# Query-weight means taken off by GpSimd, three loads on ScalarE's queue, key weights on two queues, and a new order

## The chip, the core and the metric

The kernel runs on one core of a Trainium2 chip. The core has five engines with separate instruction streams: TensorE (PE: matmuls and transposes into PSUM), VectorE (DVE), ScalarE (ACT), GpSimd (POOL) and SyncE (SP), which here only issues DMAs. ScalarE can issue DMAs too. The metric is the device time of one execution in microseconds.

## The reference

One block of a transformer, in bf16, for 2048 tokens of width 640, with 32 heads of width 20 and a gated layer of width 1536. `ln` is a layer norm without weights.

```python
q, k, v = split_heads(ln(x) @ wqkv)
pq, pk = q @ w_phi[h], k @ w_phi[h]                 # per head, 20 x 20
phi_q = concat(softmax(pq), softmax(-pq))           # 40 features
phi_k = concat(softmax(pk), softmax(-pk))
kv, z = sum_s phi_k * v, sum_s phi_k
o = (phi_q @ kv) / (phi_q @ z + 1e-6)
h = x + o @ wo
g, u = ln(h) @ w_gate, ln(h) @ w_up
out = h + (g * u) @ w_down
```

## The kernel before

The tokens lie in 16 tiles of 128, and the width of 640 in 5 chunks of 128. The kernel is a list of operations (`Prog.op`), each with its engine, what it reads and writes, and an expected length. Each operation belongs to a named unit (`U("...")`). `ORDER` gives, for each engine, a fixed list of unit names, and each name in it stands for the next operation of that unit on that engine, in the order in which the program created them (`place`, line 216). Every engine runs its list strictly in order and waits on semaphores where an operation depends on another engine's. `place` also simulates the list with the expected lengths to choose buffers and semaphores; its landing times of DMAs (line 252) are used in that simulation alone.

The stages, with the unit names:

- **Key weights ("wk", "x0" to "x4").** The layer norm's mean is folded into the weights, and `w_phi` is multiplied into them. The rows of Wk arrive in five blocks of 128 rows (`Wnat`, lines 512 to 515, unit "in"). For each block PE sums the columns (line 662) and turns the block with five transposes (line 656). Blocks 0 and 1 are copied out raw by VectorE and ScalarE (lines 693 and 696), since the mean is known only after block 4; blocks 2 to 4 are copied out later with the mean taken off (lines 708 and 711: unit "wk" again). The rounds x0 to x4 multiply by a band matrix `Phi` (six matmuls each, line 674); x0 and x1, which used raw blocks, take a second set of six with the broadcast negative mean. `evac` (line 751) copies each round to `Wp`, by ScalarE in rounds 0, 2 and 4.
- **Value weights ("wv", "c0" to "c4").** Two loads, column sums by PE, and VectorE takes the means off.
- **Token tiles.** `xT` is x transposed by the DMA (`load_xT`: the first four tiles in unit "in", then "lT4" to "lT15"). "s0", "s2", "s4", "s8" and "s12" work out 1/std for 2, 2, 4, 4 and 4 tiles: PE and VectorE make sums, and seven small operations on GpSimd make `rs`, `nrs` and `mv`. s12 takes its squares on ScalarE from `x_all`, the untransposed x, whose last quarter is "lx3".
- **Keys and values ("k", "K", "v").** PE projects a tile (10 matmuls of 320 columns), VectorE takes the largest absolute value, ScalarE writes two exponentials; then "K": sums by VectorE, scaling by GpSimd (line 827, 2.36 us a tile).
- **Query weights ("lwq", "t0" to "t4", "wm", "y0" to "y4").** Wq arrives twice: by a plain load (lwq, into `Wnat` again) for the column means, and transposed by the DMA (t0 to t4, into `WT`). "wm": 25 one-column matmuls sum the columns, and ScalarE writes the negative means, broadcast to 128x640, into `nmu`. Each round y multiplies `WT` by `Phi` (six matmuls) and adds `nmu` times `Phi` (six more).
- **Key sums ("A0" to "A14", "Aout"), queries ("q", "Q"), numerators ("n"), Wo ("wo0" to "wo4", "h"), the gated layer ("f") and its way down ("d", "e").** PE works through these for the rest of the span. "wo" sums Wo's rows on ScalarE (line 561), "h" needs Wo and x.

There are four PSUM buffers of two banks, shared by all PE stages. DMAs of one engine leave in the order of its list; SP issues all but Wrows, the small `w_phi` load, which ScalarE issues. SP's list begins "in" x 11 (key weights, value weights, four token tiles), then token tiles, x's last quarter (lx3), more tiles, Wq transposed and plain, Wo, and the gated layer's weights.

Of the kernel before, what the change touches and what calls it, by code (L numbers as in the profile page):

```python
# [376 lines left out]
def _build(ctx, nc, A_x, A_wqkv, A_w_phi, A_wo, B_w_gate, B_w_up, B_w_down, out):  # L377
# [136 lines left out]
    for c in range(NC):  # L514
        load_wnat(1, (c, c + 1))
# [588 lines left out]
```

## Time and profile before

| what | us |
|---|---|
| median of three runs | 283.45 (283.43 to 284.15) |
| the profiled execution | 281.24 |
| span within it, first to last instruction | 279.4 |
| PE busy | 274.6 (98% of the span) |
| VectorE, ScalarE, GpSimd busy | 165.5, 133.4, 106.3 |
| granted TensorE clock | 1.00 |

Busy time by stretch of the span, in us:

| stretch | PE | VectorE | ScalarE | GpSimd | DMA share |
|---|---|---|---|---|---|
| 0 to 7 | 5.68 | 1.62 | 1.99 | 3.54 | 0.71 |
| 7 to 13.7 | 6.51 | 6.16 | 3.15 | 2.61 | 1.02 |
| 20 to 30 | 10.00 | 9.86 | 8.34 | 7.92 | 1.16 |
| 40 to 50 | 10.00 | 9.76 | 9.70 | 8.99 | 0.98 |
| 60 to 70 | 10.00 | 10.00 | 8.96 | 9.92 | 0.29 |
| 70 to 80 | 9.45 | 8.49 | 5.22 | 5.04 | 1.05 |
| 100 to 150 | 50.00 | 35.27 | 22.83 | 13.02 | 0.65 |

A matmul's end is modelled in the profile, and matmuls are pipelined, so small gaps of PE do not show. The share of the DMA engines is summed over 16 engines and can come out a little above 1. The chain of waits is followed back from the last instruction; before 13.7 us it consists of SP's DMA issues and one token tile's transfer.

### The profile page before, as it was taken

What the parts mean: (1) busy time and instruction counts of PE and PEld (TensorE: products, weight loads), DVE (VectorE), ACT (ScalarE), POOL (GpSimd) and SP (SyncE); (2) the same over time, 40 slices, a digit from 0 to 9 for tenths busy, and PEclk for the clock granted to TensorE, in tenths of its full rate; (3) what the DMA queues carried; (4) which work ended last, traced back from release to release, by engine and by line L of the source; (5) the groups of instructions that cost most, each with busy time, mean ns of one, the idle gap of its engine ahead of it and who ended that gap; (6) DMA issues with size and microseconds to landing.
All of it is one profiled execution on the core that took longest, in us unless ns stands there. A gap on an engine that the chain in (4) does not pass through costs nothing.

```text
span 279.4 us, 5540 instructions
## 1 busy us (share of the span) xinstructions
PE 274.6 (98%) x2257; PEld 187.7 (67%) x2257; DVE 165.5 (59%) x313; ACT 133.4 (48%) x227; POOL 106.3 (38%) x156
## 2 busy tenths in 40 slices
PE   8999999999999999999999999999999999999996
PEld 7777778778878888877746655676454444456773
DVE  2999999999899798688528474431141132315011
ACT  2477999998566346363271432401444342410321
POOL 5348899999620322233300680002521034000321
PEclk9999999999999999999999999999999999999999
DMA  7989989404964378946530065561210001000112
GB/s 192 166 170 140 214 125 397 137 2 94 302 78 94 74 180 150 280 99 91 122 73 2 7 136 72 116 98 45 72 49 0 0 0 49 0 0 2 70 48 72
DMA packets 65241, 28.08 MB, mean 100 GB/s; under 512 B 55744, under 2 KB 63936, under 8 KB 65216
## 3 DMA queue, kind: packets, MB, share of 16 engines
q1 hardware_dynamic: 64560, 27.70, 45.8%
q8 instruction: 18, 0.29, 0.5%
q10 hardware_dynamic: 656, 0.03, 0.2%
q14 instruction: 7, 0.06, 0.1%
HBM read 11.82 MB, written 2.62 MB: 52 GB/s over the span
## 4 chain that ended last, share of the span: by engine, by line
PE 94%; SPq 3%; DMA 2%; DVE 1%; issue 0%
PE ps L568 93%; SPq L469 2%; DMA xT<-in_A_x_dram 2%; SPq L465 1%; PE ps L480 0%; DVE outb L1010 0%; DVE KVsb L893 0%; DVE rden L927 0%; DVE KVsb L896 0%
## 5 line engine op out<-in xcount | busy, mean ns | idle before, releaser
L568 PE MATMUL ps<-phik,Wgu 128*128 128x512 bf16 (+1 forms) x600 | 107.6, 336 | 0.0
L568 PEld LDWEIGHTS ps<-phik,Wgu 128*128 128x128 bf16 x600 | 58.2, 98 | 43.6 <-DVE phik L969 1.2
L969 DVE TENSOR_TENSOR phik<-ps,gate 128x512 bf16<-128x512 f32 (+1 forms) x60 | 34.0, 575 | 61.2 <-PE ps L568 60.3
L568 PE MATMUL ps<-Wp,xT 128*128 128x320 bf16 x480 | 68.4, 299 | 0.0
L967 ACT ACTIVATE gate<-ps 128x512 bf16<-128x512 f32 (+1 forms) x60 | 30.1, 512 | 70.4 <-PE ps L568 56.5
L568 PE MATMUL ps<-vaug,phik 128*128 128x320 bf16 (+3 forms) x544 | 60.2, 270 | 0.0
L568 PEld LDWEIGHTS ps<-Wp,xT 128*128 128x128 bf16 x480 | 46.2, 98 | 17.1
L568 PEld LDWEIGHTS ps<-vaug,phik 128*128 128x128 bf16 x544 | 43.4, 97 | 15.9
L985 POOL TENSOR_TENSOR outb<-t,x_all 128x640 bf16<-128x640 f32 x12 | 16.8, 1397 | 88.0 <-ACT t L982 85.7
L827 POOL TENSOR_TENSOR phik<-phik,Rk 128x1280 bf16<-128x1280 bf16 x16 | 37.3, 2357 | 0.7 <-DVE nb L809 0.6
L982 ACT ACTIVATE t<-ps,mh,rs 128x640 f32<-128x640 f32 x12 | 10.6, 882 | 41.4 <-PE ps L568 41.4
L806 DVE TENSOR_REDUCE ps<-ps 128x1 f32<-128x640 f32 x32 | 26.2, 819 | 3.5 <-PE ps L568 3.1
L846 DVE TENSOR_REDUCE Sq<-eq 128x64 f32<-128x1280 bf16 x16 | 23.5, 1474 | 1.6 <-ACT eq L813 1.6
L824 DVE TENSOR_REDUCE Ssum<-phik 128x64 f32<-128x1280 bf16 x16 | 23.4, 1471 | 0.1
L857 POOL TENSOR_TENSOR eq<-eq,rq 128x640 bf16<-128x640 bf16 x16 | 20.3, 1270 | 0.9
L852 POOL TENSOR_TENSOR rq<-Sq,rq 128x32 f32<-128x32 f32 x16 | 4.0, 255 | 39.8 <-DVE rq L851 39.8
L813 ACT ACTIVATE eq<-ps,nb,rs 128x640 bf16<-128x640 f32 x16 | 14.1, 883 | 10.1 <-DVE nb L809 9.3
L813 ACT ACTIVATE phik<-ps,nb,rs 128x640 bf16<-128x640 f32 x16 | 14.0, 884 | 3.1 <-DVE nb L809 3.0
L561 ACT ACTIVATE junk<-x_all 128x640 bf16<-128x640 bf16 x20 | 14.7, 735 | 0.0
L833 ACT ACTIVATE vaug<-ps,rs 128x640 bf16<-128x640 f32 x16 | 12.8, 801 | 3.5 <-PE ps L568 3.5
L813 ACT ACTIVATE eq<-ps,nb,nrs 128x640 bf16<-128x640 f32 x16 | 14.1, 882 | 0.0
L946 DVE SCALAR_TENSOR_TENSOR x_all<-ps,mh,x_all 128x640 bf16<-128x640 f32 x16 | 13.9, 874 | 0.4
(83 smaller groups left out, 226.4 us busy)
## 6 DMA issues: line engine op xcount, KB each, us to landing
x_all<-in_A_x_dram SPq DMA_DIRECT2D x4, 640.0 KB, 9.0
out_dram<-outb SPq DMA_DIRECT2D x15, 160.0 KB, 1.8
Wgu<-in_B_w_up_dram SPq DMA_DIRECT2D x1, 1920.0 KB, 11.3
...
phiqT<-in_A_wqkv_dram SPq DMA_DIRECT2D x5, 160.0 KB, 3.8
...
```

What stands on the lines that cost most here:

```text
L561: g.op("ACT", lambda e: e.activation(out=junk[:, v.i, :], in_=in_, func=func, accum_out=acc), rd=rd, wr=wr, use=[v], t=0.73, lat=0.97)
L568: ins = e.matmul(o_, lhsT=l_, rhs=r_, start=s_, stop=p_, skip_group_check=True)
L806: g.op("DVE", lambda e: e.tensor_reduce(out=mx(), in_=PS[v.i][:, :, 0:HALF], axis=AX.XY, op=ALU.max, apply_absolute_value=True, negate=Tru ...
L813: g.op("ACT", lambda e, s=s, sc=sc: e.activation(out=signed(dst(), s), in_=PS[v.i][:, :, 0:HALF].rearrange("p b (h f) -> p b h f", f=DH), ...
L824: g.op("DVE", lambda e: e.tensor_reduce(out=Ssum[:, vs.i, :], in_=x, axis=AX.X, op=ALU.add), rd=R_phik[t], wr=vs.R, use=[vs], t=1.39, lat=1.5)
L827: g.op("POOL", lambda e: e.tensor_tensor(out=x, in0=x, in1=Rk[:, vr.i, :].unsqueeze(2).to_broadcast([P, 2 * H, DH]), op=ALU.mult), rd=vr.R ...
L846: g.op("DVE", lambda e: e.tensor_reduce(out=Sq[:, vs.i, :], in_=eq[:, b.i, :].rearrange("p (g f) -> p g f", f=DH), axis=AX.X, op=ALU.add), ...
L857: return e.tensor_tensor(out=x, in0=x, in1=rq[:, vr.i, :].unsqueeze(2).to_broadcast([P, H, DH]), op=ALU.mult)
L946: g.op("DVE", lambda e: e.scalar_tensor_tensor(out=xv, in0=PS[v.i][:, :, 0:HALF], scalar=mh[:, t:t + 1], in1=xv, op0=ALU.subtract, op1=ALU ...
L967: g.op("ACT", lambda e: e.activation(out=gate[:, vg.i, 0:P * n], in_=PS[v.i][:, 0, 0:P * n], func=ACT.Copy), rd=[v.R[0]], wr=vg.R, use=[v, ...
L969: g.op("DVE", lambda e: e.tensor_tensor(out=hhT[:, hb, ft, sl], in0=PS[v.i][:, 1, 0:P * n], in1=gate[:, vg.i, 0:P * n], op=ALU.mult), rd=[ ...
L985: g.op("POOL", lambda e: e.tensor_tensor(out=outb[:, vo.i, :], in0=t32[:, v3.i, :], in1=x_all[:, t, :], op=ALU.add), rd=v3.R + [R_h[t]], w ...
```

## The change

- **Query means.** "wm" on ScalarE now writes five numbers per partition (`nmeanq`) instead of the 128x640 broadcast; five new GpSimd operations wq0 to wq4 add them to the transposed Wq in place. The rounds y lose their second set of six matmuls.
- **Loads.** Wo ("lwo"), the plain Wq ("lwq") and the last quarter of x ("lx3") are issued by ScalarE instead of SP.
- **Key weights.** Five loads of one block become four: blocks 0, 1 and 4 by SP, blocks 2 and 3 together by ScalarE.
- **Planner.** A load may be given its landing time (`at`); other expected lengths of DMAs are adjusted.
- **Order.** All six lists are new. The first entries of each that matter here are shown; the rest keeps the stages and mixes their units anew.

```diff
-                land = max(s + 2.3, fabric) + o.bytes
+                land = o.at or max(s + 2.3, fabric) + o.bytes
...
-    for c in range(NC):
-        load_wnat(1, (c, c + 1))
-    load_wv(0, 2)
-    load_wv(2, 5)
+    load_wnat(1, (0, 1), at=3.0)
+    load_wnat(1, (2, 4), "ACT", at=4.8)
+    load_wnat(1, (1, 2), at=3.7)
+    load_wnat(1, (4, 5), at=5.3)
+    load_wv(0, 2, 6.2)
+    load_wv(2, 5, 7.8)
...
-        g.op("ACT", lambda e: e.activation(out=nmu[:, :, :], in_=PS[v.i][:, 0, 0:NC].unsqueeze(2).to_broadcast([P, NC, P]),
-                                           func=ACT.Copy, scale=-1.0 / SC), rd=[v.R[0]], wr=[R_nmu], use=[v], t=0.61, lat=0.75)
+        g.op("ACT", lambda e: e.activation(out=nmeanq[:, :], in_=PS[v.i][:, 0, 0:NC], func=ACT.Copy, scale=-1.0 / SC),
+             rd=[v.R[0]], wr=[R_nmu], use=[v], t=0.1, lat=0.23)
+        for a in range(NC):
+            U("wq%d" % a)
+            pool_op(lambda e, a=a: e.tensor_scalar(out=WT[:, 0, a, :], in0=WT[:, 0, a, :], scalar1=nmeanq[:, a:a + 1], scalar2=None,
+                                                   op0=ALU.add), 0.75, rd=[R_nmu, R_WT[0][a]], wr=[R_WT[0][a]])
...
-        g.op("PE", lambda e: mms(e, part(WT[:, 0, :, P * i:P * (i + 1)], first) + part(nmu, first)), rd=R_WT[0] + R_Phi + [R_nmu],
+        g.op("PE", lambda e: mms(e, part(WT[:, 0, :, P * i:P * (i + 1)], first)), rd=R_WT[0] + R_Phi,
...
-    load_wnat(0)
+    load_wnat(0, eng="ACT")
...
-    load(Wo[:, :, 0:D], A_wo.rearrange("(c p) n -> p c n", p=P), R_Wo, 0.8)
+    load(Wo[:, :, 0:D], A_wo.rearrange("(c p) n -> p c n", p=P), R_Wo, 0.8, eng="ACT")
```

The first entries of the lists before and after:

```diff
 PE
-"warm wk wk wk wk wk wk wk wk wk wk x1 wv x1 x0 x3 wv x0 s0 s0 x2 x4 k0 k0 k0 s2 k0 k0 s2 k1 k3 v1 k2 s4 s4 s4 s4 "
+"warm wk wk wk wk wk wk wk wk wk wk x1 wv x1 x2 x3 wv x0 x0 s0 x4 s0 k0 k0 k0 k0 k1 k0 s2 s2 k2 v1 s4 s4 s4 s4 k3 "
 ACT
-"in wk wk wk in x0 x2 x4 k0 k0 k1 v1 k1 k3 k3 k2 s12 k2 v5 k4 k4 v6 k6 k6 v3 k7 k5 k7 k5 s12 wm v4 v11 k8 k8 v10 "
+"in lwo lx3 wk in wk wk in x2 x0 x4 wo0 s12 lwq s12 k0 k0 v1 k1 k1 k2 k2 s12 wm k3 v2 k3 k4 k4 k7 k5 k5 k7 v0 k6 "
 POOL, the second line of its list
-"s4 s4 in s4 s4 s4 K1 K0 K3 s8 s8 s8 s8 s8 s8 K2 K4 K6 s12 K5 K8 s12 s12 s12 s12 s12 s2 s0 K9 K10 K7 K14 K11 Q1 "
+"in s4 s4 s4 K0 s4 s4 wq3 s4 K1 s8 wq0 s8 wq4 s8 wq2 s8 wq1 s8 s8 K4 K2 s12 s12 s12 s12 K3 s12 K5 s12 K6 K7 K10 "
 SP
-"in in in in in in in in in in in lT4 lT5 lT7 lT6 lx3 lT8 lT11 lT10 lT9 lT15 t0 lT13 lwq t3 lT12 t2 t4 t1 lT14 "
+"in in in lT5 in in in in in in lT6 lT7 lT4 lT11 t0 t3 lT10 lT8 lT9 t4 t2 t1 lT14 lT15 lT12 lT13 lu lx0 Q0 Q0 Q1 "
```

More of the change, by code (lines that the diff above doesn't have):

```diff
@@ L135 @@
     __slots__ = ("eng", "idx", "emit", "deps", "dma", "waits", "vc", "signal", "tick", "sem", "val",
-                 "n", "dur", "lat", "bufs", "succ", "start", "end", "open", "bytes", "unit")
+                 "n", "dur", "lat", "bufs", "succ", "start", "end", "open", "bytes", "unit", "at")
 class Prog:
@@ L151, in __init__, with op @@
         self.order = {}
-    def op(self, eng, emit, rd=(), wr=(), app=(), dma=None, t=0.2, lat=None, use=(), after=(), size=0.0):
+    def op(self, eng, emit, rd=(), wr=(), app=(), dma=None, t=0.2, lat=None, use=(), after=(), size=0.0, at=0.0):
         o = Op()
+        o.at = at
         o.eng, o.emit, o.dma = eng, emit, dma
@@ L421, in _build @@
     nmean = sb([P, NC], FP32, "nmean")
+    nmeanq = sb([P, NC], FP32, "nmeanq")
     Ssum = sb([P, 2, 2 * H], FP32, "Ssum")
@@ L431, in _build @@
     WT = pq[:, NC * D:3 * NC * D].rearrange("p (w a n) -> p w a n", w=2, a=NC)
-    nmu, nmuk = [outb[:, k, :].rearrange("p (a n) -> p a n", a=NC) for k in range(2)]
+    nmuk = outb[:, 1, :].rearrange("p (a n) -> p a n", a=NC)
     vaug = BV[:, :].rearrange("p (t h e) -> p t h e", t=NT, h=H)
@@ L462, in _build, with load, transpose @@
     R_hT, R_oT, R_hhT = [regs(4) for _ in range(2)], [regs(4) for _ in range(2)], [[regs(4) for _ in range(NF)] for _ in range(2)]
-    def load(out_, in_, wr, mb, after=(), eng="SP", app=()):
-        return g.op(eng, lambda e: e.dma_start(out_, in_), wr=wr, app=app, after=after, dma=("w", 8), t=0.5, lat=0.4, size=mb / 0.38)
-    def transpose(out_, in_, rd, wr, use=(), t=1.27, size=1.07):
-        return g.op("SP", lambda e: e.dma_start_transpose(out_(), in_()), rd=rd, wr=wr, use=use, dma=("tr", 8), t=t, lat=0.5,
+    def load(out_, in_, wr, mb, eng="SP", at=0.0):
+        return g.op(eng, lambda e: e.dma_start(out_, in_), wr=wr, dma=("w", 8), t=0.5, lat=0.4, size=mb / 0.38, at=at)
+    def transpose(out_, in_, rd, wr, use=(), t=1.27, size=1.07, lat=0.5):
+        return g.op("SP", lambda e: e.dma_start_transpose(out_(), in_()), rd=rd, wr=wr, use=use, dma=("tr", 8), t=t, lat=lat,
                     size=size)
@@ L494, in U, with load_wnat, load_wv @@
         g.unit = name
[L498 removed]
+    def load_wnat(w, cs=(0, NC), eng="SP", at=0.0):
         c0, c1 = cs
         load(Wnat[:, c0:c1, :], A_wqkv[P * c0:P * c1, D * w:D * (w + 1)].rearrange("(c p) n -> p c n", p=P), R_Wnat[c0:c1],
[L501 removed]
+             0.16 * (c1 - c0), eng=eng, at=at)
     def load_xT(t):
[L504 removed]
+        transpose(lambda: xT[:, t, :, 0:P], lambda: A_x[0, P * t:P * (t + 1), :], [], [R_xT[t]], t=1.3, size=0.75, lat=1.25)
     def load_x(b):
[L507 to L510 removed]
+        load(x_all[:, 4 * b:4 * b + 4, :], A_x[0, 4 * P * b:4 * P * (b + 1), :].rearrange("(t p) n -> p t n", p=P), [R_x[b]], 0.64,
+             eng="ACT" if b == NB - 1 else "SP")
+    def load_wv(c0, c1, at):
+        load(Wp[:, c0:c1, 2 * D:3 * D], A_wqkv[P * c0:P * c1, 2 * D:3 * D].rearrange("(c p) n -> p c n", p=P), R_Wp[2][c0:c1], 0.16 * (c1 - c0), at=at)
     U("in")
[L513 to L517 removed]
+    load(Wrows[:, :, :], A_w_phi.rearrange("h d f -> (h d) f").rearrange("(a p) f -> p a f", p=P), [R_Wrows], 0.03, eng="ACT", at=3.3)
+    load_wnat(1, (0, 1), at=3.0)
[4 more added lines that the diff above has]
+    load_wv(2, 5, 7.8)
     for t in range(4):
@@ L1019, in wqT @@
         U("t%d" % a)
-        transpose(lambda: WT[:, 0, a, :], lambda: A_wqkv[:, P * a:P * (a + 1)], [], [R_WT[0][a]], t=1.27, size=1.4)
+        transpose(lambda: WT[:, 0, a, :], lambda: A_wqkv[:, P * a:P * (a + 1)], [], [R_WT[0][a]], t=1.5, size=0.75, lat=1.25)
     U("warm")
```

9 lines of the change are left out of this document (1 added, 8 removed), and 78 rows, old and new, of the table ORDER.

## The prediction

> **What bounds the kernel now.** I read the page's busy lines and slices, then the chain of waits in order of time, then the timeline of the first 16 us, then the DMA issues and the GpSimd timeline up to 80 us.
>
> From the page and from the chain in order of time (start, length, what):
>
> ```profile
> PE 274.6 (98%) x2257; PEld 187.7 (67%) x2257; DVE 165.5 (59%) x313; ACT 133.4 (48%) x227; POOL 106.3 (38%) x156
> ...
> 9.02 4.64 DMA xT<-in_A_x_dram
> 13.65 0.05 issue
> 13.70 62.00 PE ps L568 x670
> ...
> 85.88 190.10 PE ps L568 x1312
> ```
>
> TensorE (PE) never waits from 13.70 to 276.0 us but for 0.9 us around 76 us (the handover from the key sums to the first numerators). Counting columns at the rate of the L568 rows gives about 260 us of true work for these 262 us, so the busy figure is real here. What is lost at the head is not won back, and what is saved can come only from the head, from PE's own work, or from that 0.9 us.
>
> The head, from its timeline (start, length, engine, line):
>
> ```profile
> 3.97 0.69 PE L656 MATMUL ps<-ident,phiqT 128*128 128x128 bf16 x5
> ...
> 5.37 0.70 ACT L696 ACTIVATE phiqT<-ps 128x640 bf16<-128x640 bf16 x1 [2.81 <-PE ps L656]
> ...
> 6.78 0.44 PE L656 MATMUL ps<-ident,phiqT 128*128 128x128 bf16 x5
> ...
> 7.27 0.48 PE L568 MATMUL ps<-Phi,phiqT 128*128 128x140 bf16 x6
> ...
> 8.45 0.79 PE L568 MATMUL ps<-Phi,phiqT 128*128 128x140 bf16 x12
> ...
> 13.70 0.28 PEld L568 LDWEIGHTS ps<-xT 128*128 128x128 bf16 x5 [0.47 <-DMA xT<-in_A_x_dram]
> ```
>
> The five row blocks of the key weights are turned (L656) as they land: the last turn ends at 7.2 us. ScalarE's first copy (L696) needs only block 1, and runs from 5.37 to 6.07. The last wait is for the token tile xT at 13.65. Two windows of the head (busy per engine, clock, DMA share, GB/s):
>
> ```profile
> 2.50:7.00 4.50, 4.22 (x64) 3.96 (x62) 1.62 (x7) 0.76 (x2) 1.94 (x11) 1.00 1.00 274
> 7.00:10.00 3.00, 2.95 (x38) 2.31 (x36) 2.55 (x6) 1.15 (x3) 0.76 (x2) 1.00 1.17 236
> ```
>
> The DMA engines are full there already, at 274 GB/s with plain loads.
>
> **The change, part by part.**
>
> *Where the second part of the key weights stands.* This decides my forecast. Blocks 2 and 3 become one load on ScalarE's queue, created as ScalarE's second "in" operation. ScalarE's list is "in lwo lx3 wk in wk wk in": names are taken in the order of creation, so the first "in" is Wrows, the second is this load, the third the Exp warm-up. It thus stands behind Wo (800 KB), a quarter of x (640 KB) and the first "wk", which is the L696 copy. A DMA issue cannot go before that copy, so it leaves at about 6.1 us (5.37 + 0.70) instead of 1.7 and 2.2. That the planner sees nothing of it follows from the diff: a load with `at` lands at 4.8 whenever it is issued. PE's list is fixed: the turns of blocks 2 to 4 come next, and behind them x, wv, s0 and every key.
>
> When does it land (T)? The quickest landing of a 160 KB load of the same weights:
>
> ```profile
> phiqT<-in_A_wqkv_dram SPq DMA_DIRECT2D x1, 160.0 KB, 2.5
> ```
>
> So T is at least 6.1 + 2.5 = 8.6 us. Its queue must also carry 1.44 MB before it, 1.76 MB with it. Data flow from about 3.2 us (issue at 1.25, and of the 2.5 us some 0.6 is the moving of 160 KB). Alone at 274 GB/s that is 6.4 us, T = 9.6. In equal shares with SP's queue, which has some 0.3 MB of key weights, 0.8 MB of value weights and token tiles to move, it is 12.8 us, T = 16. I take 12: SP's tiles move in short packets (55744 of 65241 are under 512 B), so ScalarE's longer rows should get more than half.
>
> From T to the steady state: six small PE steps (three means, three turns) 1.2 us at the later rate; 1.2 us until the late copies are done (7.2 to 8.35 now); x1, x2, x3 0.9; wv's second half 0.8; two x0 0.6; s0, x4, s0 0.9; k0 1.4. That is k0 done at T + 7.0. At 13.70 the present kernel has all this behind it and one tile of s2 (0.3), so T + 7.3 stands against 13.7: break-even at T = 6.4, and T = 12 **costs 5.6 us** (2.2 at T = 8.6, 9.6 at T = 16). Nothing covers it: all else that PE could do stands behind in its list.
>
> *PE after the gap.* PE would idle some 6 us. The turns took 0.69 us at 3.97 and 0.44 at 6.78, though the granted clock is 1.00 in both windows. If the rate falls back in the gap, three turns lose 0.25 each and the x rounds a little less: 0 to 1.5 us, I take **0.7**.
>
> The Trainium skill (TensorE: Matmul & The Clock Gate, Part 1) says that an idle window of about 3.4 us halves the array's clock until a busy one has passed. By that rule the gap would cost up to 1.7 us, an estimate from that page of the Trainium skill; no row here has such a gap.
>
> *Scales for the first keys.* rs of tiles 0 and 1 takes from s0's sums (11.10) to 13.56 now, while PE waits for tiles anyway. Afterwards s0 comes right before k0, and ScalarE has wo0 and s12 (0.95 us each by the L561 rows) ahead of k0's exponentials. k0, k1 and k2 then hold three of four PSUM buffers and PE stops: 0 to 1.6 us, I take **1.0**.
>
> *Mean matmuls gone from the query rounds.* Twelve L568 matmuls with Phi took 0.79 us, six 0.48: six cost 0.31, five rounds **1.55 us** of PE. ScalarE's 0.71 us broadcast (L725) becomes a 128x5 activate, next to the 0.20 us of L785; ScalarE is not on the chain: 0.
>
> *GpSimd's five subtractions.* No such row: 128x640 with one operand and a broadcast (L686) took 0.72, with two bf16 operands (L857) 1.27. So 3.6 to 6.4 us; one tensor operand is nearer to the first. Its cover:
>
> ```profile
> 65.04 6.99 POOL L827 TENSOR_TENSOR phik<-phik,Rk 128x1280 bf16<-128x1280 bf16 x3
> ...
> 71.72 3.97 PE L568 MATMUL ps<-vaug,phik 128*128 128x84 bf16 x100
> ```
>
> GpSimd is 90 to 99% busy from 30 to 70 us, and its last key scaling ends at 72.0; PE reads that in A14 at about 74.0. That leaves 2.0 us of slack and, of 24.9 to 72.0, some 1.6 us of idle time. 3.6 us just fits, 6.4 leaves 2.8 of waiting. As PE also arrives 1.55 earlier, a part of that gain goes into waiting for GpSimd: together **-1.0** (from -1.55 to +1.3). They also stand between s8's small operations: scales for tiles 8 to 11 come 3 us later, behind 6 us of VectorE's own list, so nothing.
>
> *Loads moved.* SP is freed of three issues (0.81 + 0.58 + 0.59); token tile 5 moves ahead of the value weights (one transpose, 1.3 us on SP against one issue of 0.46 saved twice): value weights are asked for 0.4 us later, which T covers. Wq is asked for after s12, at about 19 us; by its 6.0 us it lands at 25, before "wm" on PE at about 28, so 0; if it came later, GpSimd's wq3 would hold K1 and s8 behind it. Wo and x are needed from 44 us and 22 us on now: their early landing gains nothing. Planner's figures (`lat`, `size`, `at`) emit nothing.
>
> The Trainium skill speaks against a second queue as well (DMA: Bandwidth & Descriptors, Issuing engines are not separate DMA queues): queues of different engines share the same 16 engines and interleave, and only issue time is saved. By it the 1.44 MB come off SP's rate; the full share of 1.00 in the window above agrees.
>
> *Sum:* 5.6 + 0.7 + 1.0 - 1.0 = **+6.3 us**. The profiled execution took 281.24, 2.2 below the median; added to the median of 283.45 this is 289.7.
>
> **The rivals.**
>
> 1. *ScalarE's queue runs nearly unshared* (20%): T = 9, head +2.6, clock 0.3, scales 0.5, -1.0: 285.9. For it: 397 GB/s in the page's seventh slice. Against: the full DMA share.
> 2. *The tiles starve* (15%): packets alternate, a 256 B one of a tile against a 1280 B row, T = 15 and tiles 0 to 3 late too: 8.6 + 0.7 + 1.0 - 1.0 and 1.2 of waiting at s2: 294.
> 3. *GpSimd becomes the bound* (8%): 1.27 us per subtraction, +1.3 for -1.0: 292.0.
> 4. *The other side: the late load is covered* (7%). At 13.7 PE waits for tiles, not weights, and the new list asks for only two tiles before k1. If T is under 7.9 (6.4 + 1.55), the saved matmuls win; without the wait at 76 us too, 281.5. Against: 8.6 is the earliest landing by the rows. The case that ScalarE's list is not run as written falls here.
>
> **How the numbers follow.** Half for the forecast, with its own range of 286.5 to 293 (T from 9.6 to 15). The likeliest time is 289.7. The range, 284.5 to 295.5, takes in T = 8.6 (283.45 + 2.2 + 0.3 - 1.55 is 284.4) and rival 2. A difference of 0.3% (0.85 us) is what a measurement can tell. Faster: rival 4, 0.07. Same: the quick end of rival 1 with no loss of clock, 0.05. Slower: 0.88.
>
> **What would show it.** Right: the issue of the 320 KB load behind L696 at about 6 us; a PE gap of 4 us or more ended by that DMA; L656 turns in a second group; PE steady from about 18 to 20 us; five GpSimd operations near 0.75 us; L568 with Phi down by 30 matmuls. Wrong: turns of blocks 2 and 3 before 8 us, or the gap ended by tiles and no later than 14 us, or a new wait for GpSimd before the numerators of over 2 us.

## The result, and the profile after

| | median, us | lowest to highest | runs |
|---|---|---|---|
| before | 283.44 | 281.68 to 284.15 | 6 |
| after | 296.68 | 294.48 to 298.43 | 6 |

The changed kernel is slower: ratio 1.0477, 95% interval 1.0412 to 1.0543, or +13.2 us by the medians. The forecast was 289.7 (+6.3), with a range that ended at 295.5. The profiled execution of after took 298.31 us, one of the longer of its six, with a span of 296.6; before it was 281.24 and 279.4. The two profiles are thus 17 us apart where the medians are 13 apart, and sizes taken from them alone come out somewhat high. Ratios, here and below, leave disturbed runs out, so that one can differ a little from that of the medians (it does for c2).

From the page of after, the busy time of each engine and two rows of the 40 slices:

```profile
PE 278.3 (94%) x2227; PEld 189.0 (64%) x2227; DVE 165.7 (56%) x313; ACT 133.2 (45%) x227; POOL 116.4 (39%) x161
...
PE   6099985999999999999999999999999999999996
...
PEclk9999996899999999999999999999999999999999
```

PE runs 30 matmuls fewer (2257 to 2227) and yet is busy 3.7 us longer, in a span 17.2 longer. A slice is 7.4 us. The hole is in slice 2, a dent in slices 6 and 7, and the granted clock falls in slices 7 and 8. Everything from slice 9 on looks as before.

The chain of waits in order of time (start, length, what):

```profile
1.24 3.58 DMA phiqT<-in_A_wqkv_dram
...
5.76 8.88 DMA phiqT<-in_A_wqkv_dram
...
16.87 12.86 PE ps L573 x132
...
35.18 1.92 POOL phiqT L734
...
46.25 1.88 POOL phiqT L734
...
48.17 43.73 PE ps L573 x450
91.91 0.02 issue
91.93 0.58 DVE KVsb L902
...
127.22 165.92 PE ps L573 x1082
```

Two things that were never on the chain stand on it now: the late load of key weights, 5.76 to 14.64, and GpSimd's subtractions (L734), 35.2 to 48.1. The handover from the key sums (KVsb) was at 75.73 and is at 91.93, 16.2 later; PE's last matmul ends 17.2 later. So nearly all is lost before the key sums end, and none of it comes back.

The head, from its timeline (ACTq is ScalarE's DMA issue; in brackets the idle time before, and what ended it):

```profile
1.29 0.55 ACTq L467 DMA_DIRECT2D Wo<-in_A_wo_dram  x1
...
1.87 0.55 ACTq L467 DMA_DIRECT2D x_all<-in_A_x_dram  x1
...
5.76 0.70 ACT L701 ACTIVATE phiqT<-ps 128x640 bf16<-128x640 bf16 x1 [2.03 <-PE ps L661]
5.76 0.37 ACTq L467 DMA_DIRECT2D phiqT<-in_A_wqkv_dram  x1
...
14.69 0.29 PE L573 MATMUL ps<-ones,phiqT 128*128 128x1 bf16 x5 [8.97 <-DMA phiqT<-in_A_wqkv_dram]
...
14.85 0.69 PE L661 MATMUL ps<-ident,phiqT 128*128 128x128 bf16 x5
```

Blocks 2 and 3 are asked for behind Wo, x and ScalarE's first copy, at 5.76, and PE stands still for 9.0 us until they land at 14.64. The turns behind the gap take 0.69 us again, not 0.44. The key projections begin only at 22.41. The new list puts k1 between k0 and s2; without k1, k0 and one tile of s2 would be done at 24.05 (22.41, 1.36 for k0's ten projections, 0.28 for the tile), where before they were done at 13.70. So the head loses about 10.3 us in this execution.

PE's timeline around the first query round (y3):

```profile
39.20 5.61 PE L573 MATMUL ps<-Wp,xT 128*128 128x320 bf16 x40 [0.93 <-ACT phik L822]
48.17 0.78 PE L573 MATMUL ps<-Phi,phiqT 128*128 128x140 bf16 x6 [3.37 <-POOL phiqT L734]
48.75 2.87 PE L573 MATMUL ps<-Wp,xT 128*128 128x320 bf16 x10
...
51.59 2.68 PE L573 MATMUL ps<-Wp,xT 128*128 128x320 bf16 x10
...
57.20 0.48 PE L573 MATMUL ps<-Phi,phiqT 128*128 128x140 bf16 x6
57.52 1.52 PE L573 MATMUL ps<-Wp,xT 128*128 128x320 bf16 x10
```

PE waits 3.37 us for the last subtraction. Behind the gap the same work takes nearly twice as long (0.78 for 0.48, 2.87 and 2.68 for 1.52) until 54.3, the end of the second row of ten projections: 0.3 + 1.35 + 1.16, some 2.8 us more. At 57.5 it is back at 1.52. Three windows (busy of PE, PEld, VectorE, ScalarE, GpSimd; granted clock; DMA share; GB/s):

```profile
7.00:13.70 6.70, 0.00 (x0) 0.00 (x0) 0.00 (x0) 0.00 (x0) 0.00 (x0) 1.00 1.09 249
...
40.00:50.00 10.00, 6.63 (x47) 4.55 (x45) 5.30 (x9) 5.98 (x10) 9.78 (x10) 0.86 0.85 278
50.00:60.00 10.00, 10.00 (x85) 6.87 (x83) 7.43 (x11) 7.23 (x12) 8.95 (x9) 0.80 0.02 6
```

In the gap of the head no engine computes while the DMA engines are full. The 1.00 of the first row is no measurement: the trace of after has no clock record before 19.85 us, and a stretch without a record counts as 1.00. From 40 to 60 us the clock is 0.86 and 0.80 (in narrower windows 0.50 from 47.16 to 53.98 and 1.00 around that), and GpSimd is the busy engine. The five subtractions by tile (shortest, mean, longest in ns; when; shapes):

```profile
L734 POOL TENSOR_SCALAR phiqT<-phiqT,nmeanq x5: 1885/1892/1918, 35.2 to 46.2; 128x640 bf16<-128x640 bf16 x5
```

1.89 us each, not 0.72 to 1.27.

### The profile page after: what moved, and what is told of

Its sections match the earlier page's. It is cut to its first block, busy times and chain, and to the rows that moved or that the text cites. A ratio compares the mean times of both kernels' runs of the same rounds, so it can differ in the third digit from the quotient of the medians.

```text
span 296.6 us, 5487 instructions
## 1 busy us (share of the span) xinstructions
PE 278.3 (94%) x2227; PEld 189.0 (64%) x2227; DVE 165.7 (56%) x313; ACT 133.2 (45%) x227; POOL 116.4 (39%) x161
## 4 chain that ended last, share of the span: by engine, by line
PE 81%; DMA 8%; POOL 6%; DVE 1%; SPq 1%; ACT 1%; issue 0%; ACTq 0%; DVEq 0%; POOLq 0%
PE ps L573 81%; DMA phiqT<-in_A_wqkv_dram 4%; POOL phiqT L734 3%; DMA vaug<-ob 3%; POOL phik L836 2%; DMA phiqT<-eq 1%; SPq L471 1%; PE ps L661 1%; ACT eq L822 1%; POOL rs L629 0%; DVE outb L1019 0%; DVE ob L938 0%; DVE t L617 0%; DVE KVsb L902 0%; POOL vpe L627 0%
## 5 line engine op out<-in xcount | busy, mean ns | idle before, releaser
L573 PE MATMUL ps<-Wp,xT 128*128 128x320 bf16 x480 | 71.9, 306 | 0.9 <-ACT phik L822 0.9
L961 POOL TENSOR_SCALAR vpe<-shc 128x1 f32<-128x1 f32 x16 | 3.1, 192 | 46.2 <-ACT junk L566 45.3
```

Of the source, the lines that this page charges most:

```text
L573: ins = e.matmul(o_, lhsT=l_, rhs=r_, start=s_, stop=p_, skip_group_check=True)
```

## The experiments

Three theories stood after the profiles. **Late**: blocks 2 and 3 come late because of where they stand in ScalarE's list. **Sharing**: Wo and x, asked for at 1.3 us, take the DMA engines from whatever PE needs next, so that mending the place of one load makes another one late. **GpSimd**: the subtractions hold y3 up, and cost what they hold it up, and the slow matmuls behind, less the mean matmuls saved. All distances below are between medians, each to the kernel before as measured beside it on the same chip (281.9 to 282.5 us); after stands at +13.2. In the code, `...` stands for lines left out; what a kernel has in common with one shown before (the old means, the four loads of key weights, a unit taken out of SP's list) is named in words and not printed again.

### Undoing one part of the change

**a1_first**: blocks 2 and 3 second in ScalarE's list, before Wo and x.

```diff
-        "in lwo lx3 wk in wk wk in x2 x0 x4 wo0 s12 lwq s12 k0 k0 v1 k1 k1 k2 k2 s12 wm k3 v2 k3 k4 k4 k7 k5 k5 k7 v0 k6 "
+        "in in lwo lx3 wk wk wk in x2 x0 x4 wo0 s12 lwq s12 k0 k0 v1 k1 k1 k2 k2 s12 wm k3 v2 k3 k4 k4 k7 k5 k5 k7 v0 k6 "
```

> The changed kernel with ScalarE's list beginning in, in, lwo, lx3, wk instead of in, lwo, lx3, wk, in: the load of key-weight blocks 2 and 3 is issued second, ahead of Wo and x. Theory (the late issue, with Wo and x ahead of it, makes the 9 us gap of PE): the gap before the turn of block 2 goes, blocks 2 and 3 land by 7 us, PE is steady 8 us earlier, and the GpSimd wait before y3 stays: 288 to 289 against 296.7. Rival (Wo and x take bandwidth from the tiles on SP's queue, whichever load goes first): token tiles 0 and 1 land no earlier than 16 us, PE only steady at about 20: 292 to 294.

293.26 us, ratio 1.0385 [1.0337, 1.0433], +11.1: only 2.1 less than after. Its timeline of PE:

```profile
5.84 0.28 PE L573 MATMUL ps<-ones,phiqT 128*128 128x1 bf16 x5 [0.51 <-DMA phiqT<-in_A_wqkv_dram]
...
12.40 1.25 PE L573 MATMUL ps<-Wp,ones 128*128 128x320 bf16 x4 [4.64 <-DMA Wp<-in_A_wqkv_dram]
```

The key weights are in time and PE now waits 4.6 us for the value weights. Sharing was the theory that expected this (292 to 294), though it named token tiles as the load that is late; it was the value weights.

**a2_oldmeans**: the query means as before, all else as in after.

```diff
-        "in s4 s4 s4 K0 s4 s4 wq3 s4 K1 s8 wq0 s8 wq4 s8 wq2 s8 wq1 s8 s8 K4 K2 s12 s12 s12 s12 K3 s12 K5 s12 K6 K7 K10 "
+        "in s4 s4 s4 K0 s4 s4 s4 K1 s8 s8 s8 s8 s8 s8 K4 K2 s12 s12 s12 s12 K3 s12 K5 s12 K6 K7 K10 "
...
-            pool_op(lambda e, a=a: e.tensor_scalar(out=WT[:, 0, a, :], in0=WT[:, 0, a, :], scalar1=nmeanq[:, a:a + 1], scalar2=None,
...
-        g.op("PE", lambda e: mms(e, part(WT[:, 0, :, P * i:P * (i + 1)], first)), rd=R_WT[0] + R_Phi,
+        g.op("PE", lambda e: mms(e, part(WT[:, 0, :, P * i:P * (i + 1)], first) + part(nmu, first)), rd=R_WT[0] + R_Phi + [R_nmu],
```

> The changed kernel with the query means as before: broadcast by ScalarE, six more matmuls in each y round, no subtraction on GpSimd; all lists otherwise as changed. Theory (five subtractions of 1.89 us on GpSimd hold y3 and s8's scales, which makes the PE gap of 3.4 us before y3, a wait of 0.9 us and half-rate matmuls behind it for 3.1 us): PE runs on through 39 to 55 us, 1.55 us of matmuls come back: 290 to 291.5 against 296.7. Rival (PE waits there because Wq, now on ScalarE's queue behind s12, and the turned Wq arrive late): the wait before y3 stays within 1 us and the total is 297.5 to 298.5.

291.3 us, ratio 1.0311 [1.0252, 1.037], +9.2: 4.0 less than after. There is no wait at y3, and the clock is full behind it. That GpSimd's subtractions cost time is shown; the size is good to about 2.5 us, by the intervals of the two kernels.

**a3_both**: both edits together.

```diff
-        "in lwo lx3 wk in wk wk in x2 x0 x4 wo0 s12 lwq s12 k0 k0 v1 k1 k1 k2 k2 s12 wm k3 v2 k3 k4 k4 k7 k5 k5 k7 v0 k6 "
+        "in in lwo lx3 wk wk wk in x2 x0 x4 wo0 s12 lwq s12 k0 k0 v1 k1 k1 k2 k2 s12 wm k3 v2 k3 k4 k4 k7 k5 k5 k7 v0 k6 "
...
-        "in s4 s4 s4 K0 s4 s4 wq3 s4 K1 s8 wq0 s8 wq4 s8 wq2 s8 wq1 s8 s8 K4 K2 s12 s12 s12 s12 K3 s12 K5 s12 K6 K7 K10 "
+        "in s4 s4 s4 K0 s4 s4 s4 K1 s8 s8 s8 s8 s8 s8 K4 K2 s12 s12 s12 s12 K3 s12 K5 s12 K6 K7 K10 "
```

> Both edits at once: key-weight blocks 2 and 3 issued second by ScalarE, and the query means as before. Theory: the two losses are separate and add up: 296.7 - 8 - 6 = 282 to 283.5, level with before, with Wo, x and Wq still early on ScalarE's queue. Rival (sharing of the DMA engines): 286 to 289, with PE waiting for token tiles in the first 20 us.

289.22 us, ratio 1.0243 [1.0187, 1.0299], +7.1. The four kernels (after 13.2, a1 11.1, a2 9.2, a3 7.1) add up: lateness alone 2.1 with either form of the means, GpSimd 4.0 with either place of the load. The 4.0 are clear of the intervals, the 2.1 only just when both pairs are taken together. That they add up to a tenth is luck: beside after the kernel before took 283.44 us, beside the other three 282.12, and against 282.12 after would stand at +14.6, with steps of 3.4 to a1 and 5.4 to a2. The pairs a1, a3 and a2, a3 share one reference. PE still waits 4.6 us for value weights and 1.7 for tokens.

**a4_backlog**: the load of blocks 2 and 3 stays behind ScalarE's copy, but Wo and x go behind it.

```diff
-        "in lwo lx3 wk in wk wk in x2 x0 x4 wo0 s12 lwq s12 k0 k0 v1 k1 k1 k2 k2 s12 wm k3 v2 k3 k4 k4 k7 k5 k5 k7 v0 k6 "
+        "in wk in lwo lx3 wk wk in x2 x0 x4 wo0 s12 lwq s12 k0 k0 v1 k1 k1 k2 k2 s12 wm k3 v2 k3 k4 k4 k7 k5 k5 k7 v0 k6 "
```

> The changed kernel with ScalarE's list beginning in, wk, in, lwo, lx3: the load of blocks 2 and 3 still goes after ScalarE's first copy, but ahead of Wo and x. It parts the late issue from the queue ahead of it. Theory: issue stays at about 5.3 to 5.8 us, landing moves from 14.6 to about 9 us; the gap of PE shrinks from 9 to 3 or 4 us: 291 to 292. If the late issue alone made the loss, landing stays above 12 us and the total above 295.

296.04 us, ratio 1.0454 [1.0383, 1.0525], +13.9: no gain that can be told from after. PE's timeline:

```profile
12.17 0.29 PE L573 MATMUL ps<-ones,phiqT 128*128 128x1 bf16 x5 [6.84 <-DMA phiqT<-in_A_wqkv_dram]
...
44.98 0.49 PE L573 MATMUL ps<-Phi,phiqT 128*128 128x140 bf16 x6 [3.35 <-POOL phiqT L734]
45.30 1.52 PE L573 MATMUL ps<-Wp,xT 128*128 128x320 bf16 x10
```

Issued at 5.38, the load lands at 12.17 with only the small Wrows ahead of it on its queue: 6.8 us instead of 8.9. Its own queue's backlog is worth 2.1 us of landing. It was expected to land at about 9; that the other transfers in flight take the rest from it is likely, but no run shows it apart. And here a gap of 3.35 us before y3 is followed by work at full rate: the slow matmuls of after do not follow from the gap's length alone. This profile is of the fastest of a4's four executions (292.74 us, mean clock 0.988); the others took 295.9 to 296.4 at a mean clock of 0.971, so what the profile shows to be saved is not in the median.

**a6_away_oldmeans**: as a3, with Wo and x asked for after ScalarE's copies of the key weights.

```diff
-        "in lwo lx3 wk in wk wk in x2 x0 x4 wo0 s12 lwq s12 k0 k0 v1 k1 k1 k2 k2 s12 wm k3 v2 k3 k4 k4 k7 k5 k5 k7 v0 k6 "
+        "in in wk wk wk in lwo lx3 x2 x0 x4 wo0 s12 lwq s12 k0 k0 v1 k1 k1 k2 k2 s12 wm k3 v2 k3 k4 k4 k7 k5 k5 k7 v0 k6 "
```

> The changed kernel with the query means as before, blocks 2 and 3 of the key weights issued second on ScalarE's queue, and Wo and x only issued by ScalarE after its last key-weight copy (in, in, wk, wk, wk, in, lwo, lx3). It differs from a3_both in that place alone. Theory (1.44 MB of Wo and x on the same 16 DMA engines delay the value weights and token tiles by some 5 us): PE has no wait for Wp at 7.8 us, k0 starts at about 12 to 13 us instead of 18.0, total 283 to 284.5 against 289.2. Rival (splitting the loads over two queues, or the new order itself, costs the 7 us): 288 or more.

285.38 us, ratio 1.0116 [1.0073, 1.0159], +3.2. From a3 to a6 3.9 us are won, the price of the two loads in the head; 283 to 284.5 us were expected if these loads were all that a3 still loses. k0 starts at 13.76, before at 11.73.

### One part alone, put into the kernel before

**b1_two_queues**: four loads of key weights on two queues, both early.

```diff
-    for c in range(NC):
-        load_wnat(1, (c, c + 1))
+    load_wnat(1, (0, 1))
+    load_wnat(1, (2, 4), "ACT")
+    load_wnat(1, (1, 2))
+    load_wnat(1, (4, 5))
...
-        "in wk wk wk in x0 x2 x4 k0 k0 k1 v1 k1 k3 k3 k2 s12 k2 v5 k4 k4 v6 k6 k6 v3 k7 k5 k7 k5 s12 wm v4 v11 k8 k8 v10 "
+        "in in wk wk wk in x0 x2 x4 k0 k0 k1 v1 k1 k3 k3 k2 s12 k2 v5 k4 k4 v6 k6 k6 v3 k7 k5 k7 k5 s12 wm v4 v11 k8 k8 v10 "
```

> The kernel before with key-weight blocks 2 and 3 as one load of ScalarE's, issued second on its queue at about 1.25 us, four loads instead of five. It is b5_late without the lateness. If the lateness is what b5 pays for (5.4 us), this is within 0.8 us of before. If the one load of 320 KB on a queue of its own lands late beside SP's loads, 284 or more, with PE waiting for it at 5 to 7 us.

281.46 us against 281.87, ratio 0.9996 [0.9966, 1.0026]. The second queue neither costs nor gains.

**b5_late**: the same four loads, that of blocks 2 and 3 behind ScalarE's copy.

```diff
-        "in wk wk wk in x0 x2 x4 k0 k0 k1 v1 k1 k3 k3 k2 s12 k2 v5 k4 k4 v6 k6 k6 v3 k7 k5 k7 k5 s12 wm v4 v11 k8 k8 v10 "
+        "in wk in wk wk in x0 x2 x4 k0 k0 k1 v1 k1 k3 k3 k2 s12 k2 v5 k4 k4 v6 k6 k6 v3 k7 k5 k7 k5 s12 wm v4 v11 k8 k8 v10 "
```

> The kernel before with another part alone: key-weight blocks 2 and 3 as one load of ScalarE's, behind ScalarE's first copy, nothing else ahead of it on that queue. By the formula of the prediction (T + 7.3 against 13.7): issue near 5.3, landing T near 8.5 to 9.5, so 2 to 3 us more: 284.5 to 286. Rival (PE waits for tiles until 13.65 anyway, so the late block is covered): within 0.8 us of before.

287.93 us, ratio 1.0202 [1.0161, 1.0243], +5.4. PE's timeline:

```profile
11.00 0.29 PE L570 MATMUL ps<-ones,phiqT 128*128 128x1 bf16 x5 [6.06 <-DMA phiqT<-in_A_wqkv_dram]
```

Issued at 4.99, 320 KB land at 11.0 beside SP's value weights and tiles. With 11.0 the formula T + 7.3 against 13.7 gives +4.6, and +5.4 was measured: the forecast's way of costing a late load holds. The expectation had put T at 8.5 to 9.5 and so the loss at 2 to 3 us: what was too small was T, not the price of lateness. The place in the list alone is worth 5.4 us where nothing else is late.

**b4_loads**: Wo and the last quarter of x by ScalarE, ahead of its copies.

```diff
-        "in wk wk wk in x0 x2 x4 k0 k0 k1 v1 k1 k3 k3 k2 s12 k2 v5 k4 k4 v6 k6 k6 v3 k7 k5 k7 k5 s12 wm v4 v11 k8 k8 v10 "
+        "in lwo lx3 wk wk wk in x0 x2 x4 k0 k0 k1 v1 k1 k3 k3 k2 s12 k2 v5 k4 k4 v6 k6 k6 v3 k7 k5 k7 k5 s12 wm v4 v11 k8 k8 v10 "
```

> The kernel before with one part of the change alone: Wo and the last quarter of x are issued by ScalarE right after Wrows, and leave SP's list. Theory (1.44 MB on the second queue take their share of the same 16 DMA engines from the value weights and the token tiles): PE waits for Wp or xT some 5 us longer in the first 20 us: 287 to 289 against 282.5. Rival (in the order of before, the tiles hide it, or the loads fill DMA time that was idle): 282 to 284.

286.61 us, ratio 1.0144 [1.01, 1.0188], +4.1. Nothing that PE needs early was moved, and yet PE's timeline has

```profile
7.25 0.29 PE L568 MATMUL ps<-ones,phiqT 128*128 128x1 bf16 x5 [2.45 <-DMA phiqT<-in_A_wqkv_dram]
...
9.32 0.30 PE L568 MATMUL ps<-ones,phiqT 128*128 128x1 bf16 x5 [1.23 <-DMA phiqT<-in_A_wqkv_dram]
```

SP's key weights come later for the bytes on the other queue. The Trainium skill (DMA: Bandwidth & Descriptors, Issuing engines are not separate DMA queues) says that queues of different engines share the same 16 DMA engines; these waits of 2.45 and 1.23 us agree.

**b6_gpsimd**: only the query means, taken off by GpSimd.

```diff
-        "s4 s4 in s4 s4 s4 K1 K0 K3 s8 s8 s8 s8 s8 s8 K2 K4 K6 s12 K5 K8 s12 s12 s12 s12 s12 s2 s0 K9 K10 K7 K14 K11 Q1 "
+        "s4 s4 in s4 s4 s4 K1 K0 K3 s8 s8 s8 s8 s8 s8 wq0 wq3 K2 wq2 wq4 wq1 K4 K6 s12 K5 K8 s12 s12 s12 s12 s12 s2 s0 K9 K10 K7 K14 K11 Q1 "
```

> The kernel before with the third part alone: query means taken off in place by GpSimd (tensor_scalar), put between s8 and the scaling of key tiles 2, 4 and 6. Theory (1.89 us each, 9.4 us on an engine that is 90 to 99% busy there): y4 waits some 4 to 5 us and key scaling is late again before the key sums, less 1.55 us: 286 to 289. Rival (the order of the changed kernel, not the operations, made the wait): 281.5 to 283.

291.41 us, ratio 1.0316 [1.0272, 1.036], +8.9. PE's timeline:

```profile
47.16 1.38 PE L569 MATMUL ps<-Phi,phiqT 128*128 128x140 bf16 x12 [4.79 <-POOL phiqT L730]
...
50.15 2.85 PE L569 MATMUL ps<-Wp,xT 128*128 128x320 bf16 x10
```

A wait of 4.8 us and slow matmuls behind it. In the old order, where two GpSimd key scalings more stand ahead of them, the subtractions cost more than in the new one, and more than the 286 to 289 us that were expected.

**b2_dve_means**: the same on VectorE.

```diff
-        "K1 K0 k4 K1 k4 k6 K3 k6 k7 K3 k7 K2 k5 K2 k5 s8 s8 s8 s8 s8 K4 k8 K4 K6 k8 K5 k9 K6 k9 K8 k10 K5 k10 s12 K7 K8 "
+        "K1 K0 k4 K1 k4 k6 K3 k6 k7 K3 k7 K2 k5 K2 k5 s8 s8 s8 s8 s8 K4 k8 K4 K6 k8 K5 k9 K6 k9 K8 k10 K5 k10 wq0 wq3 wq2 wq4 wq1 s12 K7 K8 "
...
+            g.op("DVE", lambda e, a=a: e.tensor_scalar(out=WT[:, 0, a, :], in0=WT[:, 0, a, :], scalar1=nmeanq[:, a:a + 1], scalar2=None,
+                                                   op0=ALU.add), t=0.3, lat=0.4, rd=[R_nmu, R_WT[0][a]], wr=[R_WT[0][a]])
```

> The kernel before with the query means taken off in place by VectorE (0.38 us each in c1_away_dve), ahead of s12 in its list; six matmuls fewer in each y round. If PE alone bounds this stretch, 1.55 us come back: 280.5 to 281.5, faster than both kernels. If VectorE (98% busy from 20 to 50 us) is as much the bound, its 1.9 us eat the gain: 282 to 283.5.

282.91 us against 282.49, ratio 1.0022 [0.9995, 1.005]. 0.38 us for each subtraction, but PE waits 1.33 us for VectorE at the first round: the 1.55 us of saved matmuls are given back, since VectorE is as full there as PE.

### The price of the subtraction

Two kernels stand on a6's loads, with the subtraction in other forms. **c1_away_dve** puts it on VectorE (its list gets "wq3 wq0 wq4 wq2 wq1" behind K4); **c2_away_tt** leaves it on GpSimd as a two-operand instruction with the means broadcast.

```diff
-            pool_op(lambda e, a=a: e.tensor_scalar(out=WT[:, 0, a, :], in0=WT[:, 0, a, :], scalar1=nmeanq[:, a:a + 1], scalar2=None,
-                                                   op0=ALU.add), 0.75, rd=[R_nmu, R_WT[0][a]], wr=[R_WT[0][a]])
+            g.op("DVE", lambda e, a=a: e.tensor_scalar(out=WT[:, 0, a, :], in0=WT[:, 0, a, :], scalar1=nmeanq[:, a:a + 1], scalar2=None,
+                                                   op0=ALU.add), t=0.3, lat=0.4, rd=[R_nmu, R_WT[0][a]], wr=[R_WT[0][a]])
```

> As a6_away_oldmeans, but the query means are taken off in place by five tensor_scalar operations on VectorE, at the place of s8's end in its list, instead of matmuls. Theory (the idea of subtracting in place is sound and only GpSimd's 1.89 us each was wrong): VectorE needs at most 0.8 us each (its row for 128x640 from PSUM), the 1.55 us of PE come back: 281.5 to 283, or 1 to 1.5 us under a6. Rival (VectorE is as full as PE from 30 to 75 us, so five more operations eat the gain): level with a6 or up to 2 us over it.

```diff
-            pool_op(lambda e, a=a: e.tensor_scalar(out=WT[:, 0, a, :], in0=WT[:, 0, a, :], scalar1=nmeanq[:, a:a + 1], scalar2=None,
-                                                   op0=ALU.add), 0.75, rd=[R_nmu, R_WT[0][a]], wr=[R_WT[0][a]])
+            pool_op(lambda e, a=a: e.tensor_tensor(out=WT[:, 0, a, :], in0=WT[:, 0, a, :],
+                                                   in1=nmeanq[:, a:a + 1].to_broadcast([P, D]), op=ALU.add), 1.3, rd=[R_nmu, R_WT[0][a]], wr=[R_WT[0][a]])
```

> As a6_away_oldmeans with the changed kernel's GpSimd subtractions, but as tensor_tensor additions with the means broadcast, instead of tensor_scalar. If the form of the instruction sets the 1.89 us, they take 1.27 us as the other 128x640 tensor_tensor rows do, PE waits at y3 for 1 us or less and the total is 284 to 286. If any 128x640 pass of GpSimd with two operands in that memory takes 1.9 us, PE waits 3 to 4 us as before: 288 to 290.

The subtractions of c1 by tile:

```profile
L734 DVE TENSOR_SCALAR phiqT<-phiqT,nmeanq x5: 377/381/382, 37.7 to 38.8; 128x640 bf16<-128x640 bf16 x5
```

and those of c2:

```profile
L734 POOL TENSOR_TENSOR phiqT<-phiqT,nmeanq x5: 1252/1252/1253, 27.7 to 37.3; 128x640 bf16<-128x640 bf16 x5
```

The form of the instruction sets GpSimd's price: 1.25 us as tensor_tensor, 1.89 as tensor_scalar with a per-partition operand, for the same tile and result. With 1.25 us the wait before y3 is 0.72 instead of 3.37. Neither kernel gains on a6: c1 288.27 us, ratio 1.0187 [1.0116, 1.0259]; c2 287.8, ratio 1.0115 [1.0061, 1.0169]. In c1 PE waits for tokens (2.0 and 1.6 us) and for ScalarE (1.2) instead, in c2 for tokens (1.3 and 1.6). a6 issues the same loads in the same order and has no wait for tokens above 0.7 us; why the tiles are later in c1 and c2 is not shown.

### The slow matmuls behind a gap

**f1_filler**: in after, 110 useless matmuls of 128 columns in the first gap and 50 in the second.

```diff
-        "warm wk wk wk wk wk wk wk wk wk wk x1 wv x1 x2 x3 wv x0 x0 s0 x4 s0 k0 k0 k0 k0 k1 k0 s2 s2 k2 v1 s4 s4 s4 s4 k3 "
+        "warm wk wk wk wk warm2 wk wk wk wk wk wk x1 wv x1 x2 x3 wv x0 x0 s0 x4 s0 k0 k0 k0 k0 k1 k0 s2 s2 k2 v1 s4 s4 s4 s4 k3 "
...
+    U("warm2")
+    warm(110)
+    U("warm3")
+    warm(50)
```

> The changed kernel with matmuls of no use put into PE's two gaps: 110 of 128x128 behind the turn of block 1 and 50 ahead of y3. Nothing else moves. Theory (after a gap PE runs at half rate for some microseconds: 5 turns take 0.69 instead of 0.44, 10 projections 2.7 instead of 1.36): the turns at 14.7 us take 0.44, k0 is done 1.5 to 2 us earlier, the projections behind y3 take 1.36 to 1.5: 292.5 to 294 against 296.7. Rival (the granted clock of 0.8 is a limit on power, not on idleness): no gain, 296.5 or more, and a lower granted clock.

299.68 us, ratio 1.0606 [1.0545, 1.0668]: a miss. The load landed at 15.99, 3.8 us of gap were left behind the filler, and the turns took 0.44 and then 0.70 again; the projections behind y3, for which PE waited 1.41 us more, now for ScalarE, still took 2.52. The filler also held a PSUM buffer. So the time does not settle what sets the rate.

The clock records of the traces do, as far as a reading without a run of its own can. Inside the span every stretch at 0.50 lasts 3.41, 6.83 or 10.24 us, that is one, two or three steps of 3.41 us, and it begins and ends on a grid of such steps that lies differently in each execution. These are the steps around the gap before y3 in after, in a1 and in a4 (behind the comma stands what PE was busy; the third number from the end is the clock):

```profile
43.75:47.16 3.41, 1.06 (x8) 0.53 (x6) 0.57 (x1) 1.45 (x3) 3.34 (x5) 1.00 1.00 399
47.16:50.57 3.41, 2.40 (x13) 1.61 (x14) 1.58 (x3) 1.35 (x2) 3.32 (x4) 0.50 0.67 243
...
39.83:43.24 3.41, 0.55 (x5) 0.17 (x2) 0.06 (x1) 0.94 (x3) 3.34 (x3) 1.00 0.98 287
43.24:46.66 3.42, 2.93 (x15) 1.94 (x16) 2.11 (x3) 1.89 (x3) 3.33 (x4) 0.50 1.03 404
...
39.84:43.26 3.42, 1.79 (x14) 1.07 (x11) 1.27 (x2) 2.18 (x4) 3.35 (x5) 1.00 0.88 313
43.26:46.67 3.41, 1.69 (x17) 1.31 (x18) 1.16 (x3) 0.65 (x1) 3.32 (x4) 1.00 1.03 396
46.67:50.08 3.41, 3.41 (x43) 2.61 (x41) 3.32 (x6) 3.33 (x7) 3.41 (x2) 1.00 0.15 55
```

The three gaps are equally long. In after and a1 most of the gap falls into one step, PE idles 69% and 84% of it, and the next step runs at 0.50. In a4 the gap is split between two steps, 48% and 50% idle, and the clock stays at 1.00. f1 fits: the step from 13.52 to 16.93 was 72% idle, so the first two turns ran at full rate and the third, at 16.94, at half.

### What is left: the order

a6 is 3.2 us slower than before with the means as before, and with Wo and x asked for after the key weights. Four more kernels look for that rest. All keep the old means, except c3, which takes them off on VectorE.

**a7_later_oldmeans** asks for Wo and x at about 22 us and starts s12's squares and wo0 later; **c3_later_dve** is a7 with the VectorE means of c1.

```diff
-        "in lwo lx3 wk in wk wk in x2 x0 x4 wo0 s12 lwq s12 k0 k0 v1 k1 k1 k2 k2 s12 wm k3 v2 k3 k4 k4 k7 k5 k5 k7 v0 k6 "
-        "k6 s12 v11 k8 k8 v5 wo4 k10 k10 v6 y2 k11 k11 v4 y4 y0 k9 v14 k13 k13 k9 q1 v12 wo3 q1 v13 q0 v3 q0 k15 v15 k15 "
+        "in in wk wk wk in x2 x0 x4 lwq k0 k0 v1 k1 k1 k2 k2 lx3 lwo wm k3 v2 k3 k4 k4 k7 s12 k5 k5 s12 k7 v0 k6 "
+        "k6 s12 v11 k8 k8 s12 v5 wo4 wo0 k10 k10 v6 y2 k11 k11 v4 y4 y0 k9 v14 k13 k13 k9 q1 v12 wo3 q1 v13 q0 v3 q0 k15 v15 k15 "
```

> As a6_away_oldmeans, but ScalarE issues x's last quarter and Wo only after the exponentials of key tiles 0 to 2 (about 20 us), and s12 and wo0 move behind them. If the 3 us that a6 still loses come from these two loads meeting the token tiles at 10 to 18 us, PE has no wait for xT after 15 us and the total is 282 to 283.5. If they come from the key weights on two queues, token tile 5 ahead of the value weights or another place of the new order, it stays at 284.5 to 286.

> As a7_later_oldmeans with the query means taken off in place by VectorE, its five operations spread over the list ahead of k6. If PE alone bounds this stretch: 1 to 1.5 us under a7, and under the kernel before. If VectorE is as full as PE, as b2_dve_means suggests: within 0.8 us of a7.

a7: 287.78 us, ratio 1.0199 [1.0134, 1.0264]; c3: 288.92, ratio 1.0232 [1.0176, 1.0288]. Neither is better than a6; c3 is worse, a7 by little more than the intervals. Now token tiles are late: PE waits 2.1 us for xT until 31.2 us in a7, where Wo is on its way until 30.9, and 4.2 and 0.95 in c3.

**a8_t5_behind**: a6 with token tile 5 behind tiles 0 to 3 on SP's queue.

```diff
-        "in in in lT5 in in in in in in lT6 lT7 lT4 lT11 t0 t3 lT10 lT8 lT9 t4 t2 t1 lT14 lT15 lT12 lT13 lu lx0 Q0 Q0 Q1 "
+        "in in in in in in in in in lT5 lT6 lT7 lT4 lT11 t0 t3 lT10 lT8 lT9 t4 t2 t1 lT14 lT15 lT12 lT13 lu lx0 Q0 Q0 Q1 "
```

> As a6_away_oldmeans, with token tile 5 asked for behind token tiles 0 to 3 instead of ahead of the value weights. If that tile's 1.3 us on SP and on the DMA engines is a part of what a6 still loses, value weights and tiles 0 to 3 land some 1.3 us earlier and the total is 283.5 to 284.5 against 285.4; if not, 285 to 286.

287.55 us, ratio 1.0196 [1.0163, 1.0228]: not better. PE waits 1.7 us for ScalarE's exponentials, which stand behind wo0 and s12, and ScalarE itself waits 1.1 us for Wo and 2.2 for x there.

**a10_order_only**: Wo, Wq and x back on SP, key weights in time on two queues; what is left of the change is the order of the computing units, with wm, s12 and wo0 put later to fit the loads.

```diff
-        "in in in lT5 in in in in in in lT6 lT7 lT4 lT11 t0 t3 lT10 lT8 lT9 t4 t2 t1 lT14 lT15 lT12 lT13 lu lx0 Q0 Q0 Q1 "
+        "in in in in in in in in in lT5 lT6 lT7 lT4 lx3 lT11 lT10 lT8 lT9 t0 lwq t3 t4 t2 t1 lT14 lT15 lT12 lT13 lwo lu lx0 Q0 Q0 Q1 "
...
-    load_wnat(0, eng="ACT")
+    load_wnat(0)
```

> The changed kernel with every other part undone or put in time: means as before, blocks 2 and 3 issued second on ScalarE's queue (b1 showed that this costs nothing), tile 5 behind tiles 0 to 3, and x's last quarter, Wq and Wo issued by SP again, between token tiles 4 and 15 roughly where they stood before; wm, s12 and wo0 later on PE and ScalarE. What is left is the new order of the other units. Theory (no loss is left but the loads' place): 281.5 to 283. Rival (the new order itself, which asks for s0 only behind x2, x3 and x0, costs 2 to 3 us): 284 to 285.5.

287.21 us, ratio 1.0178 [1.015, 1.0206], +5.2. From the waits of PE (total us, times, longest):

```profile
PE ps L573 <- DMA phiqT<-in_A_wqkv_dram: 2.3, 2, 1.4
PE ps L573 <- ACT phik L818: 1.4, 1, 1.4
```

k0 starts at 13.36 against 11.73, and PE waits for the key weights (0.88 us), for Wq (1.38) and for ScalarE (1.39).

So 3.2 us stay in a6, 5.9 in a7, 5.5 in a8 and 5.2 in a10, and no kernel here is faster than before. That they are the price of the order is not shown. PE's rate in the head is a rival that no run sets apart. In a6 PE waits 1.57 us for key weights and then runs a step at half rate:

```profile
7.84:11.25 3.41, 3.37 (x30) 2.78 (x28) 1.87 (x5) 1.31 (x4) 0.72 (x1) 0.50 1.18 311
```

The last turn ends 0.8 us later than in before, but the second sums of the value weights start 2.2 us later (11.36 against 9.19), so some 1.4 of the 2.0 us by which k0 starts late come with the half rate. In a8 and a10 the turns take 0.69 us up to 9.1 and 8.4 us, where in before they take 0.44 from 6.4 on.

## Why the prediction was wrong

The steps of medians split the 13.2 us into 4.0 for GpSimd's subtractions (after to a2, and a1 to a3), 2.1 for the late issue (after to a1, and a2 to a3), 3.9 for Wo and x in the head (a3 to a6) and 3.2 that stay in a6. After carries an interval of about 1.9 us to each side and a reference 1.3 us above that of a1 to a3, so this is no finer than a microsecond or two. The forecast had -1.0 for the first and +7.3 for the rest together, which came to 9.2. Thus 5.0 of the missing 6.9 us are the GpSimd term and 1.9 the rest. That the rest came so near is partly luck: its terms are not the ones that were measured, as the list shows.

- **GpSimd's five subtractions together with the mean matmuls (-1.0, with +1.3 as the worst): the step that failed.** The 30 matmuls went, as said. But the bounds of 0.72 and 1.27 us were rows of other forms of instruction, and took no account of the one that the diff names; it took 1.89, beyond both. Five of them are 5.7 us longer than at 0.75. Without these, by an estimate from these rows, the last would have ended at 48.13 - 5.7 = 42.4, before PE came to y3 at 44.8. The place was wrong too: the forecast looked for the wait at the key sums (74 us), while the first query round needs all five chunks and comes first. In the profile the term is 3.4 of waiting and 2.8 of slow matmuls less 1.55, +4.6; by the medians +4.0. Rival 3 had this mechanism, with 1.27 us a subtraction and +1.3 in all.
- **Where the second part of the key weights stands (+5.6): mechanism right, size too small.** The issue at 5.76 (said: 6.1), the gap ended by that DMA and the second group of turns all came. The issue went together with the copy, not behind it. T was 14.6, not 12: ScalarE's queue moved 1760 KB from about 3.2 to 14.6 us, 158 GB/s, a little over half of the 281 GB/s of all queues in that stretch, where T = 12 needs 205. What the forecast had wrong is the view of it as one late load: a1 shows that with this load in time the value weights are late, and b4 that the bytes of Wo and x cost 4.1 us without any late issue.
- **PE after the gap (+0.7, at most 1.5): too small.** From the landing to k0 and one tile of s2 took 9.4 us instead of 7.3, so 2.1. The forecast argued from a granted clock of 1.00 for the turns of 0.69 and of 0.44 alike; that 1.00 is no measurement, since the trace of before has its first clock record at 6.23 us, and its turns go from 0.65 at 5.76 to 0.44 at 6.38. In after the first record is at 19.85, and the work from the landing up to there has the long durations (0.69 a turn, 0.81 for six matmuls with `Phi`).
- **Scales for the first keys (+1.0):** did not happen as argued. PE does not stop behind k0, k1 and k2: from 22.4 to 38.3 us none of its rows shows a wait above 0.4 us. One wait for ScalarE, 0.93 us, comes at 39 us; its likeness to the 1.0 is luck.
- **Loads moved (0 for the rest):** right for Wq, which PE never waited for in after. Wo and x were priced only through T; their own price is the 3.9 us above.
- **Order:** the forecast costed its moves near the head one by one, and nothing for the rest. The 3.2 us of a6 have no term in it, whether they are the order's or come with PE's rate in the head.
- **Rivals.** Tiles did not starve (rival 2: no wait for xT above 0.4 us), but its T of 15 was near. The queue did not run unshared (rival 1). The late load was not covered (rival 4): lateness, bytes and subtractions each cost time alone (+5.4, +4.1, +8.9 in b5, b4, b6). These three don't add up to 13.2, probably because in after they partly hide each other and the order differs; no run shows which.
